# Mirrored score blocks: from TensorE transposes one group back to DMA transposes two groups back, in a fused gated attention and mixture-of-experts kernel

## The chip, the cores and the metric

The kernel runs on one core of a Trainium2 chip. TensorE (PE) multiplies matrices and writes to PSUM, VectorE (DVE) and ScalarE (ACT) work element by element and empty PSUM, GpSimd (POOL) issues gathers, scatters and loads that cast, and SyncE (SP) only issues DMAs. The metric is the time of one execution on the device in microseconds; three runs of the kernel before gave a median of 934.35 us (934.29 to 935.93).

## The reference

Two layers follow each other. The first is a gated attention unit without softmax, for 8 batches of 2816 tokens:

```python
scores = scale * np.matmul(z, z.transpose(0, 2, 1))   # z: (8, 2816, 64), scale = 1/2816
attn = np.maximum(scores, 0.0) ** 2
x = u * np.matmul(attn, v)                            # u, v: (8, 2816, 256)
```

Queries and keys are the same z, so scores and attn are symmetric within a batch. The second layer takes the 22528 rows of x, adds a dense two-layer network (256 to 512 to 256, relu between) to the output of one of 8 experts of the same shape. The expert of a row is the largest of 8 logits x @ w_gate, and its output is multiplied by that expert's softmax probability.

## The kernel before, in words

**Tiles.** A block is 128 tokens; a batch has nK = 22 key blocks and 22 query blocks, and 176 query blocks in all are counted by g. Query blocks are worked in groups: six per batch, of w = 2, 4, 4, 4, 4, 4 blocks (line 238), 48 groups in all. For a group n there is one tile A[n] in bfloat16: 128 keys on the partitions, 22 key blocks, up to 4 x 128 queries. Its entries are relu(score) squared. Three buffers (aA, line 73) hold these tiles, so A[n + 3] takes the place of A[n], and at any time the scores can run at most two groups ahead of the group being consumed.

**Making A.** `scores` (line 329) makes one unit from one key-block pair and four query blocks (two pairs if the group has two query blocks): two or four 64-row matmuls into a pair of PSUM banks. There are NPAIR = 3 such pairs (psS). `relu` (line 353) then offers two operations to ACT and DVE, whichever is free sooner: relu with the scale from PSUM into a float32 tile r (L361 on ACT, L363 on DVE), and the square into A (L374, L376).

**Mirrors.** Because attn is symmetric, the keys of the group before, groups[n - 1], need no scores. `mirror` (line 395) turns the 128x128 blocks of A[n - 1] by PE transposes into PSUM (tp, L403), and ACT or DVE copies them to A[n] (L411, L413). The first group of a batch has none, the second has 2 x 4 blocks, the other four have 4 x 4. The remaining keys come by scores: 6, 10, 9, 9, 9, 9 units per batch.

**Using A.** `av` (line 474) makes one query block: 22 matmuls of A's blocks with v into PSUM (L487), and then DVE multiplies by u and writes a row block of pays (`gate_x`, L505), which SP transposes by DMA to xT (L507). pays has 22 row blocks, and block g uses row g % 22. After every second matmul of `av`, `fill` (line 427) may put another piece on PE: a waiting routing job, a mirror, or a burst of two or three score units, if enough PSUM pairs are free.

**Order.** The order of PE, ACT, DVE and SP is written out by a planner in the program: `now` is PE's modelled time, `free` that of ACT and DVE, `todo` the offers with their ranks and costs; `best` picks the offer that can start first, and by rank among equals. Each engine then runs its list in order and waits at semaphores. SP's list is one queue: loads of u (L132, three buffers, four blocks ahead), xT, and turned z of the next batch (zT, L111). POOL issues the loads of v, z and weights, and the scatters.

**Routing.** Eleven blocks (fewer at the end) form one routing. LAG = 5 blocks after its last block, `routing` (line 906) puts its logits (L522) on PE, then `route_a`, two small matmuls (L552, L553), and `route_b` (line 558) on DVE, in one offer of rank 0. That gives each row its place in the list of its expert; then one block per `av` is scattered to DRAM (L602), which reads its row block of pays. These waiting scatters must be done before pays is overwritten 22 blocks later.

**Experts.** After the last block, 114 tile loads feed the expert stage (slots of `up` and `down`, L800 to L822). The change doesn't touch it, but its ring buffers take the three places of A.

Of the kernel before, what the change touches and what calls it, by code (L numbers as in the profile page):

```python
# [8 lines left out]
F32 = mybir.dt.float32  # L9
# [6 lines left out]
P = 128  # L16
# [3 lines left out]
def kernel(  # L20
# [69 lines left out]
    zero = const.tile([P, ROW // 2], F32, name="zero")  # L90
# [125 lines left out]
    def zero_fill():  # L216

        nc.vector.memset(zero[:], 0.0)
        for e in range(E):
            nc.gpsimd.dma_start(out=xs[e * CAP:e * CAP + P, :], in_=zero[:])  # L220
# [89 lines left out]
    left, turns, key_at = {}, {}, {}  # L310
    for n, (b, i0, w) in enumerate(groups):
        turns[n] = [m for m in (n - 1,) if m >= 0 and groups[m][0] == b]
        turned = {k for m in turns[n] for k in range(groups[m][1], groups[m][1] + groups[m][2])}
        ks = [k for k in range(0, nK, 2) if k not in turned]

        left[n] = [tuple(ks[x:x + 4 // w]) for x in range(0, len(ks), 4 // w)]
# [12 lines left out]
    def scores(n, units):  # L329

        open_group(n)
        b, i0, w = groups[n]
        zT = zT_of[b]
        c = w * P
        while n == 0 and z0_left and parts0[z0_left[0]][0] <= units[-1][-1] + 4:
            turn_z0(z0_left.pop(0))
        made = []
        for ks in units:
            pairs.pop(0)
            s = psS.tile([P, 2, 4 * P], F32, name="s", tag="s")  # L340
            for x, k in enumerate(ks):
                for h in range(2):
                    r = slice(h * dq, (h + 1) * dq)
                    nc.tensor.matmul(out=s[:, h, x * c:(x + 1) * c], lhsT=zT[r, k + h, :],  # L344
                                     rhs=zT[r, i0:i0 + w, :], start=True, stop=True)
            made.append((ks, s))
        now[0] += 0.2
        for ks, s in made:
            now[0] += 0.01 + len(ks) * c / 2400
            relu(n, ks, s, len(ks) * c, now[0] + 0.2)  # L350
        run(now[0])
# [43 lines left out]
    def mirror(n, m):  # L395

        open_group(n)
        (b, i0, w), (_, j0, wj) = groups[n], groups[m]
        pairs.pop(0)
        tp = psS.tile([P, wj, w, P], BF, name="tp", tag="s")  # L400
        for j in range(wj):
            for i in range(w):
                nc.tensor.transpose(out=tp[:, j, i, :], in_=A[m][:, i0 + i, j * P:(j + 1) * P],  # L403
                                    identity=ident[:])
        now[0] += wj * w * 0.056

        def copy(eng):
            dst = A[n][:, j0:j0 + wj, :w * P]
            src = tp[:].rearrange("p j i q -> p j (i q)")
            if eng == "act":  # L410
                nc.scalar.copy(dst, src)  # L411
            else:
                nc.vector.tensor_copy(dst, src)  # L413

        def done(t):
            give_pair(t + 0.1)
            for j in range(wj):
                key_at[n, j0 + j] = t + 0.2

        c = wj * w * P  # L420
        offer(now[0] + 0.2, 2, {"act": (0.12 + c / 1200, copy), "dve": (0.08 + c / 1920, copy)}, done)
        run(now[0])

    jobs = []
    flip = [0]

    def fill(n, force=False):

        if jobs and jobs[0][0] <= now[0] and room(1):
            jobs.pop(0)[1]()  # L430
            return True
        for m in range(n, min(n + 3, len(groups))):
            if left[m] or turns[m]:
                break
        else:
            return False
        if groups[m][0] not in z_there:
            return False
        t = turns[m] and can_turn(m, turns[m][0])
        can = bool(turns[m]) and t is not None and t <= now[0]  # L440
        if can and (flip[0] or not left[m]) and room(1):
            flip[0] = 0
            mirror(m, turns[m].pop(0))
            return True
        if left[m]:
            want = -(-len(left[m]) // -(-len(left[m]) // NPAIR))
            if m == 0:
                want = min(want, 1 + (len(left[0]) < 6))
            busy = sum(1 for op in todo if op[0] in (1, 4))
            if room(want) and busy <= 2:  # L450
                flip[0] = 1
                scores(m, left[m][:want])
                del left[m][:want]
                return True
        return False

    def need(n, k):

        while key_at.get((n, k), 9e9) > now[0]:
# [4 lines left out]
            ts += [t for t in (can_turn(n, m) for m in turns[n]) if t is not None and t > now[0]]  # L464
# [8 lines left out]

    def av(n, i):
        b, i0, w = groups[n]
        until(lambda: ybank[0] if ybank else None)
# [3 lines left out]
        for x in range(nK):  # L480
# [9 lines left out]
            if x % 2 == 1:  # L490
                fill(n)
            if x == nK // 2 and b * nK + i > Q1 * G:
                one_scatter()
# [8 lines left out]
    def gate_x(g, o):  # L502
# [3 lines left out]
        xT = aw.tile([P, 2, P], BF, name="xT", bufs=18)  # L506
# [51 lines left out]
    def route_b(q):  # L558
        n = sizes[q]
        oh, ex, pre = rs[q]  # L560
        se = vec("se", n)
        nc.vector.tensor_reduce(out=se, in_=ex, axis=AX.X, op=ALU.add)
        o = starts[q] % (2 * G)
        rows = pays[:, o:o + n, :]
        nc.vector.reciprocal(rows.bitcast(F32)[:, :, P], se)
        nc.vector.tensor_copy(rows.bitcast(I32)[:, :, P + 1], tok[:, starts[q]:starts[q + 1]])
        assert q != Q1 or made_first[0]
        if first_of[0] != n:

            first_of[0] = n  # L570
            nc.vector.memset(smask[:, :E * n], 1.0)
            nc.vector.memset(smask[:, :E * n].rearrange("p (e t) -> p e t", e=E)[:, :, 0], 0.0)
        tb = vec("tb", E, n)
        nc.vector.tensor_copy(tb, pre[0])
        nc.vector.tensor_add(tb[:, :, 0], tb[:, :, 0], base[:])
        inc = vec("inc", E, n)
        nc.vector.tensor_tensor_scan(
            out=inc.rearrange("p e t -> p (e t)"), data0=smask[:, :E * n],
            data1=tb.rearrange("p e t -> p (e t)"),
            initial=0.0, op0=ALU.mult, op1=ALU.add)  # L580
        nc.vector.tensor_copy(base[:], inc[:, :, n - 1])
        nc.vector.tensor_add(inc, inc, pre[1])
        nc.vector.tensor_mul(inc, inc, oh)
        pos = vec("pos", n, bufs=3)
        nc.vector.tensor_reduce(out=pos, in_=inc.rearrange("p e t -> p t e"),
                                axis=AX.X, op=ALU.add)
        rs[q] = pos
# [317 lines left out]

    def routing(q):
# [10 lines left out]
        def second():  # L917
            pairs.pop(0)
            route_pre(q)
            now[0] += 0.1  # L920
            offer(now[0] + 0.2, 0, {"dve": (2.3, lambda eng: route_b(q))}, last)
# [12 lines left out]
    def late_places(q):  # L934
        route_pre(q)
        route_b(q)
        waiting.extend(range(starts[q], starts[q + 1]))

    LAG = 5
# [70 lines left out]
```

## Time and profile before

| | us |
|---|---|
| median of three runs | 934.35 |
| profiled execution | 968.39 |
| span of its trace | 966.1 |
| PE busy | 928.4 (96%) |
| ACT busy | 753.3 (78%) |
| DVE busy | 725.6 (75%) |
| POOL busy | 458.8 (47%) |
| chain that ended last, share of PE | 82% |

The profiled execution is slower than the runs without a profile, and its parts are to be read against its own time. The granted TensorE clock was 0.992 of full speed. In groups of instructions, L487 is a line of the program, "o<-vb,A" says which tiles are written and read, then come the shape and the count, the busy time in us and the mean duration in ns of one, and after the second bar the idle time of the engine just before these instructions, with what ended it. The ends of matmuls are modelled and overlap with the next, so the start of one to the start of the next is the better measure of what PE spends. The value matmuls start at 10.5 us and end at 612 us; this is the attention stage. The expert stage takes the rest.

### The profile page before, as it was taken

The page shows a single profiled execution, that of the slowest core. Times are in us where ns is not written, and L with a number is a line of the kernel's source. Part 1 is how long each engine was busy: PE and PEld are TensorE (multiplying, and loading weights), DVE is VectorE, ACT ScalarE, POOL GpSimd, SP SyncE. Part 2 cuts the span into 40 slices and gives each one's busy share as a digit, 9 for nine tenths or more (in the row PEclk, how much of TensorE's full clock was granted, in tenths as well). Part 3 has the DMA queues.
Part 4 walks back from the last instruction along what each step waited for, and adds up shares of the span by engine and source line. Part 5 has one row for each costly group of instructions (what it writes and reads, how often), then busy time and mean ns, then how long its engine had stood idle before and what let it go on. Part 6 is the DMA issues. An engine that isn't in the chain of part 4 may idle for free.

```text
span 966.1 us, 23790 instructions
## 1 busy us (share of the span) xinstructions
PE 928.4 (96%) x8922; PEld 737.9 (76%) x8922; DVE 725.6 (75%) x1434; ACT 753.3 (78%) x920; POOL 458.8 (47%) x438
## 2 busy tenths in 40 slices
PE   8999999999999999999999989888899999999996
PEld 5577777777777777777777767776788888888885
DVE  5999999899899899899899888535564454445554
ACT  6999897898898898898898885456667777676664
POOL 2103345444435535435435444465556565656555
PEclk8999999999999999999999999999999999999999
DMA  5355687567567477567467433465444444434431
GB/s 126 90 116 106 112 146 144 112 128 148 96 134 145 101 139 148 100 129 148 101 138 141 89 85 86 87 127 114 108 113 116 112 111 121 111 94 100 90 87 42
DMA packets 188146, 109.61 MB, mean 113 GB/s; under 512 B 155774, under 2 KB 163198, under 8 KB 188032
## 3 DMA queue, kind: packets, MB, share of 16 engines
q0 software_dynamic: 27808, 55.45, 27.4%
q1 hardware_dynamic: 160224, 52.67, 25.7%
q8 instruction: 69, 1.13, 0.5%
q14 instruction: 45, 0.37, 0.2%
HBM read 61.54 MB, written 37.68 MB: 103 GB/s over the span
## 4 chain that ended last, share of the span: by engine, by line
PE 82%; issue 7%; POOL 5%; DVE 3%; DMA 1%; ACT 1%; another core or an unknown queue 1%; POOLq 0%; SPq 0%; ACTq 0%; DVEq 0%
PE o L487 43%; PE yy L808 12%; PE h_ps L800 12%; PE s L344 10%; POOL out_dram L822 5%; PE tp L403 3%; PE lg L522 1%; DMA vb<-in_v_dram 1%; DVE r L363 1%; DVE A L376 1%; DVE ring L820 0%; ACT ring L819 0%; DVE pays L505 0%; ACT r L361 0%
## 5 line engine op out<-in xcount | busy, mean ns | idle before, releaser
L487 PE MATMUL o<-vb,A 128*128 128x256 bf16 x3872 | 461.5, 273 | 4.1 <-DVE A L376 1.4
L487 PEld LDWEIGHTS <-A 128*128 128x128 bf16 x3872 | 363.5, 98 | 102.6 <-issue 59.7
L602 POOL DMA_INDIRECT xs<-pays,pi x176 | 217.3, 1235 | 296.0 <-DVE pi L601 201.1
L361 ACT ACTIVATE r<-s 128x1024 f32<-128x1024 f32 (+1 forms) x253 | 243.9, 1009 | 45.8 <-PE s L344 36.2
L374 ACT ACTIVATE A<-r 128x1024 bf16<-128x1024 f32 (+1 forms) x251 | 253.0, 1047 | 0.1
L803 ACT ACTIVATE ring<-h_ps 128x1024 bf16<-128x1024 f32 x184 | 190.1, 1033 | 80.0 <-PE h_ps L800 37.8
L363 DVE TENSOR_SCALAR r<-s 128x1024 f32<-128x1024 f32 x163 | 197.3, 1217 | 27.6 <-PE s L344 23.7
L820 DVE SCALAR_TENSOR_TENSOR ring<-yy,me,ring 128x256 f32<-128x256 f32 x184 | 87.9, 482 | 154.8 <-ACT ring L819 123.8
L822 POOL DMA_INDIRECT out_dram<-ring,me x140 | 151.9, 1085 | 102.6 <-DVE ring L820 61.1
L376 DVE TENSOR_TENSOR A<-r 128x1024 bf16<-128x1024 f32 x165 | 197.6, 1214 | 1.1 <-ACT r L361 1.1
L808 PEld LDWEIGHTS <-ring 128*128 128x128 bf16 x1472 | 143.0, 98 | 33.8 <-issue 17.3
L808 PE MATMUL yy<-w2d,ring 128*128 128x256 bf16 x736 | 110.5, 273 | 12.7 <-DVE ring L820 10.6
L344 PE MATMUL s<-zT 64*128 64x512 bf16 (+1 forms) x912 | 115.7, 361 | 1.9 <-ACT zT L175 1.2
L808 PE MATMUL yy<-ring 128*128 128x256 bf16 x736 | 110.6, 273 | 0.1
L800 PE MATMUL h_ps<-ring 128*128 128x256 bf16 (+1 forms) x912 | 98.8, 253 | 1.2 <-DVE ix L832 0.6
L800 PE MATMUL h_ps<-ring,w1d 128*128 128x256 bf16 x736 | 96.2, 274 | 1.2 <-issue 1.1
L819 ACT COPY ring<-yy 128x256 f32<-128x256 f32 x184 | 70.1, 381 | 33.6 <-PE h_ps L800 21.2
L788 DVE COPY ring<-wall 128x2048 bf16 x114 | 82.1, 736 | 10.4 <-issue 9.0
L505 DVE TENSOR_TENSOR pays<-o,ut 128x256 bf16<-128x256 f32 x176 | 75.8, 431 | 15.4 <-PE o L487 10.2
L800 PEld LDWEIGHTS <-ring 128*128 128x128 bf16 x912 | 75.5, 98 | 12.5 <-DVE ring L788 3.1
L800 PEld LDWEIGHTS <-w1d 128*128 128x128 bf16 x736 | 72.2, 98 | 10.3 <-issue 1.7
L344 PEld LDWEIGHTS <-zT 64*128 64x128 bf16 x912 | 33.1, 94 | 47.8 <-issue 31.3
(116 smaller groups left out, 411.0 us busy)
## 6 DMA issues: line engine op xcount, KB each, us to landing
ut<-in_u_dram SPq DMA_DIRECT2D x88, 256.0 KB
vb<-in_v_dram POOLq DMA_DIRECT2D x16, 384.0 KB
vb<-in_v_dram POOLq DMA_DIRECT2D x16, 320.0 KB
wall<-in_moe_w_dram POOLq DMA_DIRECT2D x16, 256.0 KB
xT<-pays SPq DMA_TRANSPOSE x176
xs<-pays,pi POOLq DMA_INDIRECT x176
zr<-in_z_dram POOLq DMA_DIRECT2D x7, 352.0 KB
out_dram<-ring,me POOLq DMA_INDIRECT x140
```

The source lines that it names most:

```text
L344: nc.tensor.matmul(out=s[:, h, x * c:(x + 1) * c], lhsT=zT[r, k + h, :], rhs=zT[r, i0:i0 + w, :], start=True, stop=True)
L361: nc.scalar.activation(r[:, :, :c], s[:, :, :c], AF.Relu, scale=1.0 / S)
L363: nc.vector.tensor_scalar(out=r[:, :, :c], in0=s[:, :, :c], scalar1=1.0 / S, scalar2=0.0, op0=ALU.mult, op1=ALU.max)
L374: nc.scalar.activation(a, r, AF.Square)
L376: nc.vector.tensor_mul(a, r, r)
L487: nc.tensor.matmul(out=o[:], lhsT=A[n][:, k, (i - i0) * P:(i - i0 + 1) * P], rhs=v_of[b][:, k, :], start=(x == 0), stop=(x == nK - 1))
L602: ins = nc.gpsimd.indirect_dma_start(out=xs, out_offset=bass.IndirectOffsetOnAxis(ap=pi[:], axis=0), in_=pays[:, g % (2 * G), :].bitcast(F ...
L800: nc.tensor.matmul(out=h_ps[:, f, hs, :], lhsT=w1(c, f), rhs=xT[:, hs, c, :], start=(c == 0), stop=(c == 1))
L803: nc.scalar.activation(h, h_ps[:].rearrange("p f h t -> p f (h t)"), AF.Relu)
L808: nc.tensor.matmul(out=y[:, k, :], lhsT=h[:, f, j * P:(j + 1) * P], rhs=w2(f), start=(f == 0), stop=(f == 3))
L820: nc.vector.scalar_tensor_tensor(out=ys, in0=y[:, 1, :], scalar=me[:, j, 0:1], in1=yd, op0=ALU.mult, op1=ALU.add)
L822: ins = nc.gpsimd.indirect_dma_start(out=out, out_offset=bass.IndirectOffsetOnAxis(ap=ids[j], axis=0), in_=ys, in_offset=None, bounds_chec ...
```

## The change

Five things are changed together.

- `mirror` is removed. The keys of the group *two* back, groups[n - 2], are now turned by SP's DMA transposes (`far_steps`), one step for each of the four query blocks of group n: rows of A[a] to columns of A[n], with a = n - 2, from SBUF to SBUF, 128 x 256 or 128 x 512 elements. The steps of group a are put into the order while `av` works on group a, at every seventh matmul from the fourth on, if the planner holds the keys for ready; for the planner they have landed 10 us after the last step. The third to sixth group of a batch have such keys, so scores make 6, 11, 10, 9, 9, 9 units per batch.
- `fill` makes bursts of three score units always (at the very start fewer), and a burst may take units from the next groups.
- `route_b` is cut in three functions, which `chain` offers to DVE one after another, with rank 0.5.
- LAG is 6 and not 5, and xT has 19 buffers and not 18.
- The tile of zeros no longer has its own place, but shares one with temporary tiles.

```diff
-        turns[n] = [m for m in (n - 1,) if m >= 0 and groups[m][0] == b]
-        turned = {k for m in turns[n] for k in range(groups[m][1], groups[m][1] + groups[m][2])}
+        far[n] = [m for m in (n - 2,) if m >= 0 and groups[m][0] == b]
+        turned = {k for m in far[n] for k in range(groups[m][1], groups[m][1] + groups[m][2])}
...
-    def mirror(n, m):
...
-                nc.tensor.transpose(out=tp[:, j, i, :], in_=A[m][:, i0 + i, j * P:(j + 1) * P],
-                                    identity=ident[:])
...
+    def far_steps(a):
+
+        n = a + 2
+        if n >= len(groups) or far[n] != [a]:
+            return []
+        (b, i0, w), (_, j0, wj) = groups[n], groups[a]
+
+        def step(i):
+            assert n - 1 in A
+            open_group(n)
+            nc.sync.dma_start_transpose(out=A[n][:, j0:j0 + wj, i * P:(i + 1) * P],
+                                        in_=A[a][:, i0 + i, :wj * P])
+            if i == w - 1:
+                for j in range(wj):
+                    key_at[n, j0 + j] = now[0] + 10.0
+
+        return [(a, lambda i=i: step(i)) for i in range(w)]
...
         if left[m]:
-            want = -(-len(left[m]) // -(-len(left[m]) // NPAIR))
-            if m == 0:
-                want = min(want, 1 + (len(left[0]) < 6))
+            want = NPAIR
+            if m == 0 and len(left[0]) > 3:
+                want = 1 + (len(left[0]) < 6)
+            units = []
+            for a in range(m, min(n + 3, len(groups))):
+                if groups[a][0] in z_there and (a == m or m > 0):
+                    units += [(a, u) for u in left[a]]
+            units = units[:want]
             busy = sum(1 for op in todo if op[0] in (1, 4))
-            if room(want) and busy <= 2:
-                flip[0] = 1
-                scores(m, left[m][:want])
-                del left[m][:want]
+            if room(len(units)) and busy <= 2:
+                for a, u in units:
+                    left[a].remove(u)
+                scores(units)
                 return True
...
+    turning = []
+
     def av(n, i):
         b, i0, w = groups[n]
+        if i == i0:
+            turning.extend(far_steps(n))
...
+            if x % 7 == 3 and turning:
+                t = can_turn(turning[0][0] + 2, turning[0][0])
+                if t is not None and t <= now[0] and turning[0][0] + 1 in A:
+                    turning.pop(0)[1]()
...
-        xT = aw.tile([P, 2, P], BF, name="xT", bufs=18)
+        xT = aw.tile([P, 2, P], BF, name="xT", bufs=19)
...
+    def chain(t, fns, then):
+
+        def done(t):
+            if fns[1:]:
+                chain(t, fns[1:], then)
+            else:
+                then(t)
+
+        offer(t, 0.5, {"dve": (0.8, lambda eng: fns[0]())}, done)
...
-            offer(now[0] + 0.2, 0, {"dve": (2.3, lambda eng: route_b(q))}, last)
+            chain(now[0] + 0.2, route_b(q), last)
...
-    LAG = 5
+    LAG = 6
```

## The prediction

> **What bounds the kernel now.** I read the engine shares first, then the chain that ended last, then stretches of the attention stage (up to about 612 us; experts fill the rest). Shares of the whole span cannot say what a mirror is worth, so the stretch from 50 to 550 us carries the argument. First its busy times, and those of 100 to 150 us:
>
> ```profile
> 50.00:550.00 500.00, 499.72 (x4900) 377.05 (x4897) 456.39 (x851) 438.81 (x468) 214.43 (x194) 1.00 0.65 126
> ...
> 100.00:150.00 50.00, 49.95 (x487) 37.19 (x485) 46.87 (x84) 47.62 (x51) 23.11 (x21) 1.00 0.75 129
> ```
>
> The columns are PE, its weight loads, DVE, ACT and POOL, then clock, DMA share, GB/s. TensorE has no holes; DVE and ACT together are at 89.5% over the long stretch and at 94.5% over the short one. PE's lines in the long stretch (busy, mean ns, idle before):
>
> ```profile
> L487 PE MATMUL o<-vb,A 128*128 128x256 bf16 x3298 | 390.9, 273 | 0.0
> L344 PE MATMUL s<-zT 64*128 64x512 bf16 (+1 forms) x786 | 98.2, 358 | 0.0
> L403 PE MATMUL tp<-ident,A 128*128 128x128 bf16 x504 | 33.9, 219 | 0.0
> ```
>
> Nothing is waited for: this stage ends when TensorE has issued everything, so work taken from it shortens it, and waits of ACT and DVE cost nothing. The busy figures overlap at their modelled ends, so I price PE from start to start, in the timeline:
>
> ```profile
> 311.90 3.01 PE L487 MATMUL o<-vb,A 128*128 128x256 bf16 x26
> 314.75 1.06 PE L403 MATMUL tp<-ident,A 128*128 128x128 bf16 x16
> 315.64 1.69 PE L487 MATMUL o<-vb,A 128*128 128x256 bf16 x14
> 317.27 0.82 PE L344 MATMUL s<-zT 64*128 64x512 bf16 x6
> 318.02 2.14 PE L487 MATMUL o<-vb,A 128*128 128x256 bf16 x18
> 320.09 0.82 PE L344 MATMUL s<-zT 64*128 64x512 bf16 x6
> ```
>
> A full mirror takes 315.64 - 314.75 = 0.89 us; a burst of three score pairs 318.02 - 317.27 = 0.75. Then the groups of the mirrors' copies:
>
> ```profile
> L411 ACT COPY A<-tp 128x2048 bf16<-128x2048 bf16 (+1 forms) x25 | 40.5, 1622 | 19.5 <-PE tp L403 19.4
> L413 DVE COPY A<-tp 128x2048 bf16<-128x2048 bf16 (+1 forms) x15 | 17.8, 1185 | 6.8 <-PE tp L403 6.8
> ```
>
> And the tiles xT and zT, with SP's transposes that exist today (least, median and greatest ns that SP takes to issue one):
>
> ```profile
> L507 SPq DMA_TRANSPOSE xT<-pays x176: 1167/1179/2998, 20.0 to 614.0; - x176
> L111 SPq DMA_TRANSPOSE zT<-zn x14: 1288/1404/2467, 55.7 to 499.7; - x14
> ```
>
> **What the Trainium skill says.** "TensorE: Matmul & The Clock Gate", section "Wait — 56ns, not 53.3ns?", gives 55.6 ns from one warm 128-column matmul to the next; the trace agrees (0.89 us / 16). "VectorE: DVE Perf Modes", "The three transpose paths", gives a DMA transpose of one 128x128 block 1309 ns. In the trace, a two-block xT has its last 256-byte packet 2.3 us after its issue began (median, 6.0 at most), queues included. "DMA: Bandwidth & Descriptors", "Latency and other measured facts", puts transposes with a non-contiguous middle dimension at 261 GB/s, so a step's 128 KB at 0.5 us (an estimate); nothing in the trace writes such a destination. Its section "Issuing engines are not separate DMA queues" says that all issuers share 16 engines; the trace has them busy 0.65 of the stretch.
>
> **The change part by part.** A batch has groups of 2, 4, 4, 4, 4, 4 query blocks.
>
> *Mirrors removed.* Per batch 8 + 4 x 16 = 72 PE transposes, 576 in all: 576 / 16 x 0.89 = 32.0 us of PE. Not all of it counts: up to about 38 us the chain runs through DVE and ACT (L363, L376), PE has holes, and that part contains 8 + 16 + 16 transposes, 2.2 us. Gain 29.8.
>
> *Scores added.* Only four groups of a batch are turned, not five: 54 score units, not 52; 16 more in all. Bursts of three and two pairs (0.75 and 0.54 us) differ by 0.21 us, so 16 x 0.22 = 3.5 us of PE lost.
>
> *Threes across groups.* A break in the value matmuls costs about 0.2 us beyond its pairs (0.1 in the burst, 0.1 in the 18 matmuls before the next, which take 2.07 us where 18 x 0.1096 = 1.97; 0.1096 is 2.85 / 26 above). Before: 3,3 / 3,3,2,2 / four times 3,3,3 = 18 bursts a batch. After: 54 / 3 = 18. I count nothing; eight bursts either way are 1.6 us.
>
> *ACT and DVE.* Copies gone: 40.5 + 17.8 = 58.3 us. Added: 16 units with a relu, (243.9 + 197.3) / 416 = 1.06 us, and a square, (253.0 + 197.6) / 416 = 1.08: 34 us. Net 24 us less over two engines, 3.0 per batch. A batch takes 73.3 us (value matmuls start at 241.2 and 314.5 for two successive ones); PE's after is 73.3 - 4.0 + 0.44 = 69.7. Load: (0.895 x 146.6 - 3.0) / 139.4 = 92%, under the 94.5% seen without a PE hole. Counting score and value matmuls in order of time, scores of a group are complete 10 to 20 us before its values begin, from the fifth group to the third-last; this lead hides the rest. Were it gone, the excess over PE would be paid in full. At the start, where they bind, groups 1 and 2 gain two units (4.3 us) and lose two copies (some 2.5): 1.8 / 2 = 0.9 us lost.
>
> *DMA transposes added.* Per batch 4 groups x 4 = 16, in all 128 (32 of two blocks, 96 of four). On SP: two blocks take 1.18 us, eleven 1.40, so four about 1.2. SP per batch: 22 x 1.18 + 11 x 0.33 (ut) + 2 x 1.40 + 16 x 1.2 = 51.6 of 69.7 us. Queued behind a waiting one are the ut loads and xT; ut now lands at least 9.7 us before its product, xT is issued at least 13 us before its logits in the long stretch, so a few us of SP delay are hidden. The turned keys have about 20 us: issued as group n - 2 starts, read as n starts, with group n - 1 (13 us) between. Engines: in 660 to 900 us the hardware queue moved 8.54 MB, nearly all transposes, in 22.2% of 240 us; 14.7 MB more are at most 92 us of 16 engines, raising the share from 0.65 to about 0.83. Below nothing it cannot cost; above, see the rivals. I take 0.
>
> *Routing in steps, LAG 6, another xT buffer, zero in a shared buffer.* The same 10 to 12 DVE instructions per routing, now letting products in between; no PE work. LAG delays each scatter by one block (3.3 us): a product (L505) must not overwrite its pays row before the scatter 22 blocks back has read it. Today the last scatter packet is 4.8 us (least; median 10.2) ahead, so 1.5 remain at worst. I take 0; the scores' lead hides small waits.
>
> *Sum.* 29.8 - 3.5 - 0.9 = 25.4 us, against the profiled execution's 968.4: 943.0, or 2.6%. That execution is 34 us above the median, and the profile doesn't say where; 2.6% of 934.35 is 24.5. Predicted 910; 904 to 916 is this case's own range (no startup loss at one end; bursts, and a PE wait of some 4 us at the other).
>
> **Rivals.** *Part is given back* (915 to 930). If ACT and DVE can't exceed today's 89.5%, a batch takes 128.2 / 1.79 = 71.6 us, the gain is 1.7 x 8 = 13.6 less the losses at the start (2.2 + 0.9): about 924. Late scatters would act alike. For it: three free pairs are now needed for every burst. Against it: the 94.5%, and scores that pause for 5 us at each batch's end for want of a free A buffer.
>
> *No change.* If PE's holes reappear one for one: 934. The zero idle speaks against it.
>
> *Slower: SP becomes the bound.* SP's time per batch is 32.4 + 16d. From d = 2.3 us it exceeds 69.7, from d = 2.6 it exceeds today's 73.3; at 3.0 a batch takes 80.4, 57 us in all: about 990. For it: the gapped destination is new, and issues of 3.0 us occur today [...]. Against it: eleven blocks cost only 1.40.
>
> **How the numbers follow.** Forecast 0.64, part given back 0.17, no change 0.03, slower 0.16. Two tenths of a per cent (1.9 us) is about what a measurement can tell, so faster 0.81, same 0.03, slower 0.16. Range 902 to 930: the first two cases with their ends.
>
> **What would show it.** PE without tp lines and still without holes in 50 to 550 us; 432 relus where there are 416; SP's new lines near 1.2 us; batches of 69 to 70 us. Wrong if PE waits for A from a DMA, if DVE's product waits for ut or a scatter, or if SP's new issues take over 2.3 us.

## The result, and the profile after

The kernel after takes 924.94 us (median of four runs; 921.77 to 929.99) where the kernel before takes 935.06 (four runs; 934.29 to 935.93): a ratio of 0.9897, with an interval of 0.985 to 0.9944. So 10.1 us were gained where 24.5 were forecast. The profiled execution of after took 925.87 us, its span is 924.1. The profile of before that the prediction read was of an execution 34 us above the median. A second one of the same kernel (the first experiment) took 935.9 us with a span of 933.9, and it is the measure for after from here on. The first had most of its excess in the expert stage: from the last value matmul to the last matmul of all it took 346.9 us, the second 324.2, after 327.0.

What SP and the relus do came as forecast. The first fence has the stretch from 50 to 550 us of the second profile of before, the next one the same stretch of after, with 50 us out of it (columns: PE, weight loads, DVE, ACT, POOL, then clock, DMA share, GB/s):

```profile
50.00:550.00 500.00, 500.00 (x4909) 377.71 (x4908) 457.92 (x855) 440.18 (x468) 215.25 (x195) 1.00 0.65 126
```

```profile
50.00:550.00 500.00, 489.36 (x4511) 357.83 (x4509) 461.20 (x867) 429.67 (x468) 216.78 (x195) 0.99 0.83 152
```

```profile
400.00:450.00 50.00, 45.93 (x402) 33.55 (x401) 39.84 (x86) 35.38 (x40) 19.71 (x19) 0.93 0.91 157
```

The DMA share is 0.83, as forecast. But TensorE has holes now, 10.6 us of them in this stretch, and from 400 to 450 us the mean granted clock is 0.93. The chain of work that ended last, which lay on PE for 82% of the second profile of before, is off PE for a third of the span:

```profile
PE 64%; issue 11%; POOL 10%; DVE 7%; DMA 5%; ACT 2%; POOLq 1%; DVEq 0%; SPq 0%; ACTq 0%
```

The 5% of DMA are scatters. The groups of the relus (281 + 151 = 432, as forecast), and then the tiles A, xT and zT with SP's issues (least, median, greatest ns):

```profile
L361 ACT ACTIVATE r<-s 128x1024 f32<-128x1024 f32 (+1 forms) x281 | 270.3, 1010 | 52.8 <-PE s L344 47.9
...
L363 DVE TENSOR_SCALAR r<-s 128x1024 f32<-128x1024 f32 x151 | 183.5, 1217 | 4.6 <-PE s L344 3.7
```

```profile
L405 SPq DMA_TRANSPOSE A<-A x128: 1175/1257/2695, 10.2 to 566.9; - x128
L501 SPq DMA_TRANSPOSE xT<-pays x176: 1167/1190/3693, 19.3 to 595.1; - x176
L110 SPq DMA_TRANSPOSE zT<-zn x14: 1382/1438/3713, 52.1 to 491.5; - x14
```

1.26 us an issue, where I took 1.2. The destination with gaps is no dearer than xT's: from the start of an issue to its last packet the median is 2.33 us for A and 2.56 for xT.

The start of one batch's value matmuls to the start of the next one's (the last: to the last value matmul), us:

| | 1 | 2 | 3 | 4 | 5 | 6 | 7 | 8 |
|---|---|---|---|---|---|---|---|---|
| before, second profile | 84.8 | 73.1 | 73.1 | 73.1 | 73.1 | 73.1 | 73.1 | 68.8 |
| after | 77.3 | 70.4 | 74.1 | 73.2 | 70.3 | 77.1 | 69.7 | 66.1 |

The seventh batch takes the forecast 69.7 us to the tenth. The third, fourth and sixth take 3.5 to 7.4 us more. The waits of after name what came between (what waited, for what: us in all, times, longest):

```profile
DVE pays L499 <- DMA xs<-pays,pi: 11.4, 10, 3.6
...
PE pre L546 <- DVE se L560: 5.1, 3, 3.9
PE o L477 <- DVE pi L604: 3.8, 5, 1.5
```

The first line is the wait that the prediction put at nothing, and had named as a sign of being wrong: the product (L499) may not overwrite its row block of pays before the scatter of 22 blocks ago has read it. In the second profile of before it isn't there. The other two are PE's waits for DVE. The last one isn't a wait for routing, though L604 belongs to the scatters: each of these five waits stands before the first value matmul of a block, which needs one of the two PSUM banks of o, and a bank is free when the product two blocks back has read it. L604 is what DVE runs right behind that product:

```profile
222.39 0.42 DVE L499 TENSOR_TENSOR pays<-o,ut 128x256 bf16<-128x256 f32 x1 [3.62 <-DMA xs<-pays,pi]
...
222.86 0.82 PE L477 MATMUL o<-vb,A 128*128 128x256 bf16 x6 [1.47 <-DVE pi L604]
```

The routing is reached in the timeline of the largest hole:

```profile
432.35 2.13 PE L477 MATMUL o<-vb,A 128*128 128x256 bf16 x18
...
436.32 0.42 DVE L499 TENSOR_TENSOR pays<-o,ut 128x256 bf16<-128x256 f32 x1 [3.64 <-issue]
...
437.96 0.38 DVE L560 TENSOR_REDUCE se<-ex 128x11 f32<-128x88 f32 x1
438.39 0.10 PEld L546 LDWEIGHTS <-ones 128*128 128x128 bf16 x1 [4.20 <-DVE se L560]
438.40 0.26 PE L546 MATMUL pre<-oh,ones 128*128 128x88 bf16 x1 [3.92 <-DVE se L560]
```

DVE stands for 3.64 us ahead of the product at 436.32. The profile names no releaser, but the semaphore that ends DVE's wait is that of the scatter issued at 427.87, whose last signal comes at 436.24, 8.4 us later. The products that wait so in after wait for slow scatters: 4.6 to 8.4 us from issue to last signal, where the median is 3.4. Slow ones are not new (up to 7.2 us in the second profile of before); what is new is that they come too near. Behind the product on DVE stands the routing, down to L560; behind that, PE's list has the small matmul L546 next, and PE waits 3.92 us for it. The scores that run ahead can't help: PE doesn't wait for A, but for a small matmul, or for a bank, further up in its own list. Four holes that end right behind a product which had waited, or behind its routing, make up 6.5 of the 10.6 us.

### The profile page after: what moved, and what is told of

It reads as the page before. It is cut to its first block, busy times and chain, and to the rows that moved or that the text cites. A ratio compares the mean times of both kernels' runs of the same rounds, so it can differ in the third digit from the quotient of the medians.

```text
span 924.1 us, 23019 instructions
## 1 busy us (share of the span) xinstructions
PE 897.6 (97%) x8378; PEld 710.7 (77%) x8378; DVE 718.8 (78%) x1432; ACT 737.1 (80%) x914; POOL 466.3 (50%) x438
## 4 chain that ended last, share of the span: by engine, by line
PE 64%; issue 11%; POOL 10%; DVE 7%; DMA 5%; ACT 2%; POOLq 1%; DVEq 0%; SPq 0%; ACTq 0%
PE o L477 32%; PE h_ps L803 11%; PE yy L811 11%; PE s L344 8%; POOL out_dram L825 8%; DMA xs<-pays,pi 5%; DVE r L363 2%; DVE A L376 2%; POOL xs L605 1%; DVE pays L499 1%; PE lg L516 1%; ACT r L361 1%; POOL vb L123 1%; PE warm L149 0%; POOLq L825 0%
## 5 line engine op out<-in xcount | busy, mean ns | idle before, releaser
L605 POOL DMA_INDIRECT xs<-pays,pi x176 | 220.4, 1252 | 275.3 <-DVE pi L604 195.3
L361 ACT ACTIVATE r<-s 128x1024 f32<-128x1024 f32 (+1 forms) x281 | 270.3, 1010 | 52.8 <-PE s L344 47.9
L374 ACT ACTIVATE A<-r 128x1024 bf16<-128x1024 f32 x242 | 246.9, 1056 | 7.4 <-DMA A<-A 2.8
L376 DVE TENSOR_TENSOR A<-r 128x1024 bf16<-128x1024 f32 (+1 forms) x190 | 225.3, 1201 | 2.9 <-issue 2.4
L363 DVE TENSOR_SCALAR r<-s 128x1024 f32<-128x1024 f32 x151 | 183.5, 1217 | 4.6 <-PE s L344 3.7
L344 PE MATMUL s<-zT 64*128 64x512 bf16 (+1 forms) x944 | 122.9, 362 | 4.9 <-ACT zT L174 2.2
L499 DVE TENSOR_TENSOR pays<-o,ut 128x256 bf16<-128x256 f32 x176 | 74.6, 424 | 32.6 <-PE o L477 14.8
L803 PE MATMUL h_ps<-ring 128*128 128x256 bf16 (+1 forms) x912 | 95.8, 252 | 0.0
L803 PEld LDWEIGHTS <-ring 128*128 128x128 bf16 x912 | 76.3, 98 | 6.8
L344 PEld LDWEIGHTS <-zT 64*128 64x128 bf16 x944 | 36.3, 94 | 56.1 <-issue 37.2
L822 ACT COPY ring<-yy 128x256 f32<-128x256 f32 x184 | 67.4, 366 | 2.1 <-PE yy L811 2.1
```

The source lines that it names most:

```text
L361: nc.scalar.activation(r[:, :, :c], s[:, :, :c], AF.Relu, scale=1.0 / S)
L363: nc.vector.tensor_scalar(out=r[:, :, :c], in0=s[:, :, :c], scalar1=1.0 / S, scalar2=0.0, op0=ALU.mult, op1=ALU.max)
L374: nc.scalar.activation(a, r, AF.Square)
L376: nc.vector.tensor_mul(a, r, r)
L605: ins = nc.gpsimd.indirect_dma_start(out=xs, out_offset=bass.IndirectOffsetOnAxis(ap=pi[:], axis=0), in_=pays[:, g % (2 * G), :].bitcast(F ...
L803: nc.tensor.matmul(out=h_ps[:, f, hs, :], lhsT=w1(c, f), rhs=xT[:, hs, c, :], start=(c == 0), stop=(c == 1))
```

## The experiments

Four theories were set against each other for the 14 us that are missing, with the numbers that they have in the expectations. The first: scatters come too late for the products, through LAG 6 and the routing in steps. The second: the bytes on the DMA engines make landings late. The third: ACT and DVE can't supply more than they do. The fourth, added after the first runs: SP's queue is so full that what stands in it behind the 128 new issues comes late.

Besides the median, four numbers are given of each run. *Holes* are the times from one matmul to the next beyond the pace of its kind, from 45 us to the end of attention. *Margin* is the time from the last packet of a scatter to the product that overwrites what it read (least and median). *Delay* is that from a product to the issue of its own scatter (median). *SP* is the time that SP issues from 50 to 550 us.

| | median us | ratio (interval) | holes | margin | delay | SP |
|---|---|---|---|---|---|---|
| before_again | 935.18 | 0.9997 (0.9984 to 1.0009) | 0.4 | 4.61, 10.21 | 60.2 | 240.7 |
| after | 924.94 | 0.9897 (0.985 to 0.9944) | 14.4 | 0.54, 3.08 | 65.8 | 405.8 |
| after_lag5 | 926.48 | 0.9891 (0.9867 to 0.9915) | 15.2 | 2.57, 6.59 | 63.4 | 397.3 |
| merged_lag6 | 922.64 | 0.9862 (0.9846 to 0.9879) | 12.0 | 0.49, 2.99 | 65.0 | 341.8 |
| merged_lag5 | 909.75 | 0.9733 (0.971 to 0.9755) | 0.3 | 0.64, 5.92 | 60.7 | 348.3 |
| merged_lag4 | 907.56 | 0.972 (0.9699 to 0.9741) | 0.3 | 3.20, 9.49 | 57.2 | 349.7 |
| merged_no_span | 909.42 | 0.9735 (0.9719 to 0.9751) | 1.3 | 4.16, 8.84 | 57.6 | 362.3 |
| merged_far_alone | 916.04 | 0.9798 (0.9782 to 0.9815) | 4.9 | 4.08, 11.03 | 55.5 | 353.8 |

**The kernel before, once more** (before_again), to have a profile near its median.

> The kernel before, unchanged, for a second profile. The first profiled execution was 34 us above the median. If the extra time lies in the expert stage and in the last blocks of attention (holes of TensorE between 560 and 700 us in the first profile), a profile near 935 us has value matmuls ending near 605 us rather than 612, with 73.3 us per batch as in the first profile. If the extra time is spread over the attention stage, batches are about 71 us here, and then the changed kernel's undisturbed batches (69.7 to 70.4 us in its profile) gain little on them.

935.18 us. The excess of the first profile lay in the last batch of attention and in the expert stage, not in the batches that the prediction was worked out on (73.3 there, 73.1 here).

**LAG back to 5** (after_lag5).

```diff
-    LAG = 6
+    LAG = 5
```

> The changed kernel with LAG back at 5; nothing else undone. Theory 1 (scatters late by the larger LAG: a product has to wait for the scatter 22 blocks back, DVE stops, then PE): the scatters come one block, some 3.2 us, earlier; DVE's product no longer waits for a scatter, all batches take 69.7 to 70.5 us instead of 70.3 to 77.0, attention is some 13 us shorter, the time 908 to 914. Theory 2 (the DMA engines, busy 0.83 of the stretch, make landings late whatever the order): less than a third comes back, 920 to 926. Theory 3 (ACT and DVE can't supply PE at the new pace): no change, 922 to 930, with holes of PE that end with a relu or a square.

926.48 us, where the first theory had 908 to 914: no gain, though the margin's median doubles and the products' waits for scatters are gone. Late scatters aren't the whole cause. Other waits have taken their place:

```profile
PE s L344 <- DMA zT<-zn: 9.6, 5, 4.2
```

These are among the first score matmuls of a batch. They need the turned z of that batch, which stands in SP's queue like everything else. SP's timeline ahead of the longest of these waits, then PE's line that ends it:

```profile
339.45 2.16 SPq L110 DMA_TRANSPOSE zT<-zn  x1
341.70 0.53 SPq L131 DMA_DIRECT2D ut<-in_u_dram  x1
342.40 1.30 SPq L405 DMA_TRANSPOSE A<-A  x1
343.75 1.23 SPq L501 DMA_TRANSPOSE xT<-pays  x1
345.03 2.58 SPq L405 DMA_TRANSPOSE A<-A  x2
347.71 3.13 SPq L110 DMA_TRANSPOSE zT<-zn  x1
```

```profile
355.63 0.39 PE L344 MATMUL s<-zT 64*128 64x256 bf16 x1 [4.17 <-DMA zT<-zn]
```

The input of the second half was ready at 341.2 us (the end of DVE's copy). SP issued it 6.5 us later, after a load and four transposes that stood ahead of it with hardly a pause; its own issue took 3.13 us, its last signal came at 355.58, and PE had stood for 4.17 us. Before the change, the second half of a batch's turned z landed 3.8 to 11.5 us ahead of the batch's first score matmul; in after 4.5 us ahead at best, and up to 3.4 us behind it. In after itself this costs little, since a few score matmuls run before the second half is needed (PE waits 0.5 us for z in all); there the waits for scatters come first.

**The loop of scatters doubled from the start** (after_two_scatters). Each `av` may put two scatters into the order and not one.

```diff
-            if x == nK // 2 and b * nK + i > Q1 * G:
+            if x == nK // 2:
```

> The changed kernel with LAG 6 kept and a second scatter per query block in all of attention, not only in its last part, so that the list of waiting scatters empties twice as fast. Theory 1: the later scatters of a routing gain margin, the first two or three do not; most of the product's waits go, time 908 to 918. Theory 2: more scatters at once in the same DMA queues, no gain or a loss, 922 to 930. Theory 3: no change.

921.18 us, ratio 0.9826 (0.979 to 0.9862). The margin is now 5.62 at least and 15.0 in the median, wider than in before, and holes of 12.3 us stay; the first theory had 908 to 918. With SP's queue as it is, early scatters bring a few us at most.

**LAG 6 in the kernel before** (before_lag6), with its xT buffer and the shared tile of zeros.

```diff
-    zero = const.tile([P, ROW // 2], F32, name="zero")
+        zero = tt.tile([P, ROW // 2], F32, name="zero", tag="o1", bufs=1)
-        xT = aw.tile([P, 2, P], BF, name="xT", bufs=18)
+        xT = aw.tile([P, 2, P], BF, name="xT", bufs=19)
-    LAG = 5
+    LAG = 6
```

> The kernel before with LAG 6, 19 xT buffers and the shared tile of zeros, which is this part of the change alone. In the first profile of before the last packet of a scatter was at least 4.8 us ahead of the product that overwrites its row; one block of 3.3 us later leaves 1.5 us. Theory 1: almost no wait yet, 934 to 938, since the margin is used up only together with shorter blocks, later landings and the stepped routing. If LAG alone costs what the changed kernel lost, 942 to 950.

943.84 us, ratio 1.0082 (1.0061 to 1.0103): a miss. Attention ends 4.4 us later and the expert stage takes 4.6 us more, though no product waits for a scatter (the margin is 2.52 at least and 6.93 in the median). So this part of the change costs time even where nothing else is changed; LAG, the xT buffer and the tile weren't separated. In attention PE has holes of 3.6 us, 1.7 of them before value matmuls that want a bank of o; what takes the 4.6 us in the expert stage stays open.

**Fewer issues for the same bytes** (merged_lag5, LAG 5; merged_lag6, LAG 6). A source group of four blocks is turned by one transpose and not four; the 128x128 blocks then lie in A[n] in another order, and `av` reads them there. 24 issues of 512 KB and 32 small ones stand where there were 128.

```diff
+        def whole():
+            assert n - 1 in A
+            open_group(n)
+            nc.sync.dma_start_transpose(
+                out=A[n][:, j0:j0 + wj, :].rearrange("p j (i q) -> p (j i) q", q=P),
+                in_=A[a][:, i0:i0 + w, :].rearrange("p i c -> p (i c)"))
+            for j in range(wj):
+                key_at[n, j0 + j] = now[0] + 10.0
+
+        if wj == 4:
+            return [(a, whole)]
...
+    def block(n, k, i):
+        b, i0, w = groups[n]
+        if far[n]:
+            _, j0, wj = groups[far[n][0]]
+            if wj == 4 and j0 <= k < j0 + 4:
+                e = (i - i0) * 4 + k - j0
+                return A[n][:, j0 + e // 4, (e % 4) * P:(e % 4 + 1) * P]
+        return A[n][:, k, (i - i0) * P:(i - i0 + 1) * P]
...
-            nc.tensor.matmul(out=o[:], lhsT=A[n][:, k, (i - i0) * P:(i - i0 + 1) * P],
+            nc.tensor.matmul(out=o[:], lhsT=block(n, k, i),
```

> LAG 5, and where the source group has four query blocks the four DMA transposes of a group are one: SP issues 56 transposes of A instead of 128, with the same bytes. (The turned blocks lie in another order within A, and the value matmuls read them there.) Theory 4 (SP's queue is too full: turned z, xT and so the logits come late behind the steps): about 40 us less of issuing on SP between 50 and 550 us, xT issued within 1 to 2 us of its product (median 2.5 us with LAG 5 now), no waits of score matmuls for turned z, batches of 69.5 to 70.5 us, time 905 to 913. Theory 2 (bytes on the DMA engines make the landings late): the bytes are the same, so 920 to 927.

> The same merged transposes with the changed kernel's LAG 6. Theory 4: SP is relieved, but scatters are one block later again, so some waits of the product for a scatter remain and the expert stage starts a little later; 3 to 8 us more than with LAG 5: 909 to 920. Theory 2: 921 to 928, as the changed kernel.

The long stretch of merged_lag5, and its tile A:

```profile
50.00:550.00 500.00, 499.91 (x4669) 368.77 (x4666) 476.22 (x914) 444.86 (x486) 226.00 (x206) 1.00 0.82 157
```

```profile
L405 SPq DMA_TRANSPOSE A<-A x32: 1175/1230/2248, 10.2 to 514.3; - x32
L414 SPq DMA_TRANSPOSE A<-A x24: 1549/2471/4347, 23.6 to 541.6; - x24
```

With LAG 5 this is the forecast: 909.75 us, no hole, batches 2 to 7 at 69.7 to 69.9 us, ACT and DVE at (476.22 + 444.86) / 1000 = 92.1%, where I had worked out 92. The DMA share is that of after (0.82), so the bytes alone don't make the holes, and the second theory falls. With LAG 6 on the same chip, 12.9 us of it are lost again, where I had expected 3 to 8, and the first theory's wait is back:

```profile
DVE pays L519 <- DMA xs<-pays,pi: 19.5, 17, 4.2
```

So there are two causes, late scatters and the 128 issues, and each alone is enough for most of the loss. LAG 5 alone (926.48) and fewer issues alone (922.64) leave some 13 to 17 us to merged_lag5; together they recover it.

**Turned z earlier** (lag5_zt_early, LAG 5): the load of z and its two transposes are put into the order two or three blocks earlier.

```diff
-            soon(t + 3, lambda b=b: load_z(b + 1))
-            soon(t + 8, lambda b=b: turn_z(b + 1, 0, nK // 2), 0.4)
-            soon(t + 9, lambda b=b: turn_z(b + 1, nK // 2, nK), 0.4)
+            soon(t + 1, lambda b=b: load_z(b + 1))
+            soon(t + 5, lambda b=b: turn_z(b + 1, 0, nK // 2), 0.4)
+            soon(t + 6, lambda b=b: turn_z(b + 1, nK // 2, nK), 0.4)
```

> LAG 5, and the load and the transposes of the next batch's z come two to three blocks earlier (blocks 1, 5 and 6 of a batch instead of 3, 8 and 9). Nothing else is relieved on SP. Theory 4: the 10 us in which score matmuls waited for turned z go, and with them some of the 6.5 us of slow clock after the holes; waits of the logits for xT (3 us) stay: 911 to 918. Theory 2: z lands late as well at the new place, 922 to 928.

923.39 us, ratio 0.9869 (0.9851 to 0.9887). The 911 to 918 expected were missed: z now lands 5.5 to 13.8 us early and nothing waits for it, but holes of 11.2 us stay. The queue makes other things late, now that z has gone ahead:

```profile
ACT A L374 <- DMA A<-A: 11.4, 5, 3.9
...
DVE A L376 <- DMA A<-A: 8.9, 5, 3.5
```

These are squares that wait to write into a buffer of A from which a transpose still reads.

**All keys by scores** (all_scores, LAG 5): no group is turned, so SP has nothing new and PE, ACT and DVE have more units.

```diff
-        far[n] = [m for m in (n - 2,) if m >= 0 and groups[m][0] == b]
+        far[n] = []
```

> The changed kernel with LAG 5 and no turned keys at all: every key by scores, 62 units a batch instead of 54, no DMA transposes of A. It shows what ACT and DVE can supply. Eight more units of 2.14 us over two engines are 8.6 us a batch more for each; with 64.1 us now that is 72.7 us if both were never idle, and 76 to 80 us at the shares seen (92 to 95%). Expected 960 to 990, with TensorE waiting for squares. If the batch takes 73 us or less, ACT and DVE have more room than assumed, and theory 3 is out.

947.74 us, ratio 1.0129 (1.0109 to 1.015), less than the 960 to 990 expected; it is the price of the units. The long stretch:

```profile
50.00:550.00 500.00, 485.15 (x4447) 346.75 (x4446) 482.72 (x872) 468.71 (x511) 206.67 (x191) 1.00 0.64 124
```

ACT and DVE are at (482.72 + 468.71) / 1000 = 95.1%, with PE waiting for them. The batches take 72.8 to 76.3 us, not all under the 73 that were to settle the third theory; the share settles it. They can supply 95%, so the 89.1% of after isn't their limit.

**The parts on top of fewer issues**, with LAG 5: no bursts across groups (merged_no_span); in merged_far_alone the routing is in one offer again as well; LAG 4 (merged_lag4).

```diff
-                if groups[a][0] in z_there and (a == m or m > 0):
+                if groups[a][0] in z_there and a == m:
...
-            chain(now[0] + 0.2, route_b(q), last)
+            offer(now[0] + 0.2, 0, {"dve": (2.3, lambda eng: [fn() for fn in route_b(q)])}, last)
```

> Merged transposes, LAG 5, stepped routing, bursts within one group. By the working of the prediction threes across groups save no bursts in a steady batch; with 10 and 11 units a group left alone is cut 3,3,3,1 and 3,3,3,2, so two more bursts a batch, 0.2 us each, some 3 us in all: 910 to 915.

> Merged transposes and LAG 5 as in the run of 909.8 us, but bursts stay within one group and the routing's second half is one offer again: of the change only the turned keys (merged) and the place of the zeros are left. If these are all that the change is worth, 908 to 914, batches of 69.7 us. If threes across groups or the steps carry part of it, 915 to 922.

> Merged transposes, LAG 4. Scatters come one block earlier still, and the expert stage's first tables too; but the logits come only 4 blocks after the last product, and xT has to be there. If SP is now free enough, 906 to 911; if xT comes late again (issued up to 6 us after its product with LAG 5), TensorE waits at logits and 912 to 920.

909.42 us without the spans (merged_lag5: 909.75): they are worth no time, as forecast, but they take 2.9 us of the median margin (8.84 without, 5.92 with). 916.04 (914.51 to 916.64) with the routing in one piece as well: the steps are worth 6.6 us here, where I had written nothing, though they take 2.2 us of the margin (11.03 without). Part of the 6.6 is again z, for which PE waits 3.3 us in two batches:

```profile
PE s L344 <- DMA zT<-zn: 3.3, 2, 2.2
```

LAG 4 gives 907.56 (907.01 to 910.5), the lowest of all; the runs don't tell it from merged_lag5, but its least margin is 3.20 and not 0.64 us, and both beat before and after.

**Steps spread over the `av`** (lag5_spread, LAG 5): two chances for a step of turning in each `av`, not three.

```diff
-            if x % 7 == 3 and turning:
+            if x % 11 == 3 and turning:
```

> LAG 5 with all 128 single transposes, but at most two steps per query block instead of three, so that the four of a group are spread over two blocks. The same issuing on SP in all, less of it in a bunch. Theory 4a (the bunching of four steps delays turned z, xT and u): 913 to 921. Theory 4b (the sum of SP's issuing, 0.80 of the time, is what counts): 922 to 928, as with LAG 5 alone (926.5).

932.5 us, ratio 0.9963 (0.9945 to 0.9981), outside both ranges and worse than after_lag5. The turning of a group ends later, and squares wait for the buffer from which it still reads; z is late as before:

```profile
ACT A L374 <- DMA A<-A: 11.2, 3, 4.8
...
PE s L344 <- DMA zT<-zn: 6.3, 2, 5.5
```

The edit moves the end of the turning as well as spreading it, and whether bunching is part of the queue's delay isn't settled by it.

**Issues whose data nobody reads** (merged_sp_load, and once more as merged_sp_load_2): merged_lag5 with three idle transposes of 128x128 after each large one, into a tile that nobody reads; xT has 18 buffers, to make room. SP gets 72 issues more, of 32 KB each.

```diff
+        def idle():
+            sc = aw.tile([P, P], BF, name="sc", bufs=2)
+            nc.sync.dma_start_transpose(out=sc[:], in_=ident[:])
+
         if wj == 4:
-            return [(a, whole)]
+            return [(a, whole)] + [(a, idle)] * 3
```

> The kernel with merged transposes and LAG 5 (909.8 us), and behind each of its 24 whole transposes three idle ones of one 128 x 128 block of the identity into a scratch tile: 72 more issues on SP of some 1.2 us, that is as many as the changed kernel has, and 2.4 MB of bytes instead of none. They leave nothing out and compute nothing. Theory 4 (SP's issuing is the cause): xT is issued late again (median 2 to 4 us after its product), score matmuls or logits wait for SP's transposes, 916 to 928. If the cause is something else in the 128 single transposes (their bytes, their semaphores on A), 908 to 912.

> The merged kernel with 72 idle transposes on SP once more, since the kernel before took 967 us on the chip of the first run, with an expert stage of 348 us where others show 325. If SP's issuing costs what that run's attention stage showed (batches of 78 to 82 us against 69.7), the time is 970 to 985 where the kernel before takes 935; if most of it came from that chip, 915 to 930.

1002.26 us on a chip on which the kernel before took 966.91, and 967.93 where it took 934.78; the ratios agree, 1.0361 (1.0283 to 1.0439) and 1.0373 (1.0325 to 1.0421). That is far over the 916 to 928 expected. Against merged_lag5's 909.75 the 72 issues cost 58 us, at 72 x 1.23 = 89 us of SP's time. The long stretch of the second run and its waits:

```profile
50.00:550.00 500.00, 460.07 (x4174) 335.25 (x4171) 427.57 (x810) 395.49 (x433) 197.71 (x183) 0.96 0.79 147
```

```profile
PE s L344 <- DMA zT<-zn: 39.8, 6, 8.1
```

Turned z comes late in six of the seven batches that need it, 6.6 us each time. The bytes in sum aren't what delays it: the share of the DMA engines is lower (0.79) than where there are no holes (0.82). Nor is it the sum of SP's issuing, 407 us here and 405.8 in after, which lost 14 us. And the idle transposes bring waits of their own: SP stands 8.9 us, in six waits from 50 to 550 us, until one of their two scratch buffers is free.

**Loads of u on another queue** (lag5_ut_pool, and once more as lag5_ut_pool_2; LAG 5).

```diff
-        nc.sync.dma_start(out=ut[:], in_=uf[:, b, i:i + 2, :])
+        (nc.sync if g < 4 else nc.gpsimd).dma_start(out=ut[:], in_=uf[:, b, i:i + 2, :])
```

> LAG 5 with all 128 single transposes, and the loads of u issued by POOL instead of SP. SP is relieved of 36 us of 500; the transposes of A are untouched. Theory 4: xT and turned z come earlier, part of the 17 us of holes goes, 915 to 923; no change or worse (924 to 932) if the loads of u now come late behind the scatters on POOL, or if SP isn't the cause.

> LAG 5, single transposes, u loaded by POOL, once more for the same reason. In the first run xT was issued 1.2 us (median) after its product, not 2.5, and turned z was in time in the first three batches, late in four. Expected by theory 4: 918 to 925; without relief 926 to 932.

Ratios of 0.9854 (0.975 to 0.9957) and 0.9943 (0.9915 to 0.997): no gain over after_lag5 is shown, though SP issues for some 345 us only, like merged_lag5. The waits of the second run, in a profiled execution of 947.48 us where the median is 930.84, so that their sizes are not to be set beside those of other runs:

```profile
PE s L344 <- DMA zT<-zn: 20.3, 4, 7.7
POOL ut L131 <- DVE pays L499: 11.2, 6, 5.5
ACT A L374 <- DMA A<-A: 8.0, 3, 6.3
```

z is still late, and POOL, which also issues the scatters, now waits for a free buffer of u. So the sum of SP's time doesn't decide by itself. That what stands in the queue ahead of z when its input is ready does, fits, but no run isolates it: the order of SP's list changed with each experiment.

**Routing in one step** (after_onestep): LAG 6 and the 128 issues as in after, with the routing as one offer of rank 0.

```diff
-            chain(now[0] + 0.2, route_b(q), last)
+            offer(now[0] + 0.2, 0, {"dve": (2.3, lambda eng: [fn() for fn in route_b(q)])}, last)
```

> The changed kernel (LAG 6, 128 single transposes, threes across groups) with the second half of the routing as one offer of rank 0 again. In the traces the last packet of a scatter is 10.2 us ahead of the product that overwrites its row before the change (median), 6.9 with LAG 6 alone, 3.1 after the change, and 11.0 against 5.9 between one offer and steps with merged transposes. So the steps took as much of the margin as LAG did. Expected: margin near 7 us again, no waits of the product for scatters; SP's delays of turned z and xT stay. If the scatters were the main loss, 912 to 919; if SP's queue is, 920 to 928.

929.43 us, ratio 0.9942 (0.9918 to 0.9966); its profile is of an execution of 920.17 us, the lowest. The delay from product to scatter falls from 65.8 to 62.2 us, the margin's median rises from 3.08 to 6.16 and none is under 1.5 us (24 of 154 were under 1 us in after), and yet nothing is gained. No product waits for a scatter any more; PE still waits for banks of o, and squares for transposes (what holds up the products that free the banks wasn't traced):

```profile
PE o L477 <- DVE pi L604: 5.2, 7, 1.2
ACT A L374 <- DMA A<-A: 5.1, 3, 2.4
```

## Why the prediction was right and wrong

**PE's part was right.** Mirrors removed and scores added give a batch of 69.7 us; undisturbed batches take 69.7. The load of ACT and DVE (92%), the count of relus, the DMA share (0.83) and the price of a new issue (1.26 us for 1.2) hold too, and the bursts across groups save no time. With both causes of loss removed, merged_lag5 has the forecast batch.

**The start was wrong in sign.** I wrote off 2.2 us of the mirrors and 0.9 us more, which leaves the first batch 0.5 us. It gained 7.5 us less 1.2 for a later first value matmul. From 10 to 50 us, DVE was busy for 34.2 us in the second profile of before and for 37.9 in after, ACT for 34.3 and 38.2. I counted only the work of the two engines, not their waits for PE, which was itself held up. The waits in that time, the first two before, the last after:

```profile
ACT r L361 <- PE s L344: 5.6, 6, 2.7
PE o L487 <- DMA vb<-in_v_dram: 2.3, 2, 1.5
ACT r L361 <- PE s L344: 1.6, 4, 0.7
```

Which of the parts reorders PE's list so isn't isolated; the turned keys aren't needed for it, as in all_scores the two engines are busy for 38.2 us each as well. The early gain hid part of the other losses, and merged_lag5's 909.75 beside my 910 owes something to this luck: it gains 6.9 us by the second batch's start, and the expert stage takes 2.9 us back.

**One step that failed is "a few us of SP delay are hidden".** I summed SP's issues to 51.6 of 69.7 us, compared them with 100%, and checked the cover of ut and xT only. Turned z, in the same queue, landed 3.8 to 11.5 us ahead of its batch's first score matmul, and I never looked; nor at squares, which must wait until a transpose has read the buffer that they overwrite. SP issued for 81% of the stretch (240.7 us became 405.8), and already so the queue is long: xT was issued 0.43 us after its product's end in before (median; 4.68 at most) and 3.56 in after (11.18). My threshold for this rival, an issue of 2.3 us, was far off: here the queue made its users late long before it was full. "DMA: Bandwidth & Descriptors", section "Issuing engines are not separate DMA queues", has it that the sequencer's time to start a DMA is usually small beside the DMA itself. Here it isn't: 1.26 us of issue stand beside the 0.5 us of data that I estimated, and merged_sp_load shows what 72 further issues can cost.

**The other is the margin of the scatters: "1.5 remain at worst", with the rest at nothing.** LAG alone was sized right: in before_lag6 the median margin falls by the 3.3 us that I wrote, from 10.21 to 6.93, and no product waits. What failed is that I counted no other loss of margin. In the runs with merged transposes it is 11.03 us with LAG 5, the routing in one offer and bursts within a group, more than before the change. The steps of the routing take 2.2 us of it (8.84), bursts across groups 2.9 (5.92), and LAG 6 another 2.9 (2.99): the scatters are issued later and later, 55.5, 57.6, 60.7 and 65.0 us after their product. In after itself, the routing in one offer gives 3.1 us back (after_onestep; its expectation sets 11.0 beside 5.9 for the steps, but those two runs differ in the bursts as well). The shorter blocks are not to blame: the delay is a number of blocks, too, and shrinks with them (60.2 us before the change). How the bursts delay the routing wasn't traced. Nor do "the scores' lead hides small waits" and "letting products in between" hold: a product that waits on DVE holds the routing behind it and a bank of o, and PE, in its own order, waits for the routing's small matmul or for the bank.

**The rival that came closest** was "part is given back (915 to 930)", where I wrote "Late scatters would act alike"; its main mechanism, a limit of ACT and DVE at 89.5%, fell.

**What stays open**: what LAG 6 costs in the kernel before; why 72 issues cost as much as 58 us; and how much is the queue's length and how much its order.

## What to carry to other kernels

A queue that only issues DMAs has to be checked like an engine: list everything in it, and for each the time by which it is early, before more is put into it; with LAG 5, fewer and larger transfers of the same bytes kept the gain that many small ones lost. When a change has several parts, take what each of them costs from every margin that it touches, those parts too that are meant to save time: here three of them took 2 to 3 us each, and the 3 us that were left are less than a slow scatter takes beyond a usual one. And a loss that has two sufficient causes shows little when either is removed alone: try the pair.

## What the runs showed of the hardware

After PE's hole of 3.92 us at 438.4 us in after, 30 value matmuls took 5.89 us. The first 23 took 0.21 us each, twice the pace of 0.11, at which the last ran again:

```profile
438.52 5.89 PE L477 MATMUL o<-vb,A 128*128 128x256 bf16 x30
```

So that hole costs 5.89 - 30 x 0.1096 = 2.6 us more, and over the attention of after such slow matmuls add 3.0 us to the 14.4 of holes. "TensorE: Matmul & The Clock Gate", section "Part 1: The HAM clock gate", says that the clock is halved after an idle window of some 3.4 us and is full again after as long a busy one. The trace agrees on the halving (the granted clock is 0.50 from 207.8 to 211.1 us in after_lag5), but not on the length of the hole. There it was halved behind a hole of 1.78 us, and not behind one of 2.09 us (26 value matmuls behind each took 4.68 and 3.00 us):

```profile
206.82 0.28 PE L344 MATMUL s<-zT 64*128 64x256 bf16 x1 [1.78 <-DMA zT<-zn]
207.03 4.68 PE L477 MATMUL o<-vb,A 128*128 128x256 bf16 x26
...
437.07 0.69 PE L516 MATMUL lg<-wg,xT 128*128 128x8 bf16 x22 [2.09 <-ACT r L361]
437.62 3.00 PE L477 MATMUL o<-vb,A 128*128 128x256 bf16 x26
```

One chip ran the kernel before in 966.91 us where others took 935, with expert stages of 347.7 and 350.8 us and not some 325 in the two kernels profiled on it, like the 346.9 of the profile that the prediction was worked out on; the ratios to before agreed within their intervals for both kernels run on both. A transpose of sixteen 128x128 blocks took SP 2.47 us to issue (median; 1.55 at least), one of four 1.26.
